# The last feed-forward's gated products by one level of Strassen's scheme, with the weights' block sums kept in DRAM

## The chip, the cores and the metric

One core of a Trainium2 chip. The metric is the device time of one execution in microseconds (us), as the median of several runs. The engines are TensorE (PE; its weight loads are shown apart as PEld), VectorE (DVE), ScalarE (ACT), GpSimd (POOL) and SyncE (SP, which only issues transfers here). They run side by side, each through its own list of instructions in order.

## The reference

Three layers follow each other on 8 x 576 = 4608 tokens of width 512: an attention over 32 memory slots, a feed-forward with 2048 hidden units, and a feed-forward with 768 hidden units, each of them the largest of three products. The last one is what changes:

```python
def _moe_ref(x, w_in, w_out):
    h = x @ w_in
    g = h - np.tanh(h)
    return (g @ w_out).astype(np.float32)

def _moe2_ref(x, w1, w2, w3, w_out):
    h = np.maximum(np.maximum(x @ w1, x @ w2), x @ w3)
    return (h @ w_out).astype(np.float32)
```

`x @ w1`, `x @ w2` and `x @ w3` are the gated products: depth 512, 768 columns each.

## The kernel before

Every 32-bit operand of a large product is split into a high part of type fp32r and the rest, and a product is three matmuls (`mm3`): high x high, high x rest, rest x high. So each factor needs two tiles, made by a copy with a cast and a subtraction.

The tanhshrink feed-forward runs in two passes over the hidden units (`ph` 0 and 1) of 8 blocks `fc` each, over tiles of 288, 320 or 512 tokens; a step is one block of one tile. For a step, `emit_h` makes the hidden values in PSUM (`ps_h`, from `at` and `vw`), `emit_g` takes `h - tanh(h)` on ScalarE and VectorE and splits it (`gh`, the subtraction on GpSimd), and `emit_x` adds its products with `wo` into four PSUM banks (`ps_x`). `emit_h` and `emit_g` run three to four steps ahead. Pass 1 adds the result of pass 0, read from DRAM into `xo`, and writes the sum to DRAM (`xd[1]`). The attention is made in pieces beside pass 0.

Weights come as 64-bit numbers. `conv` turns 512 columns of them into 32 bits: one transfer, one step on ScalarE, five on VectorE, one on GpSimd, and two more where the result is split. Such conversions are background work: `slot()` calls the generators queued in `bg` at a fixed rate per step (`rate[1]`, in quarters per slot, five slots per step). The scheduler behind the program then orders each engine's list by its own estimate of when things are ready. `Paced` ties background instructions of VectorE, ScalarE and TensorE behind the last step's instruction of that engine; GpSimd's and SyncE's are not tied.

The last feed-forward follows pass 1. It walks over nine tiles of 512 tokens. Before it, 9 of the 18 weight blocks (128 of 768 columns of one matrix) are converted during pass 1 and stored in DRAM (`wb_d`); 5 of them are loaded into pool `pre` on GpSimd's queue, the other 4 into pool `wb` as the stage begins. The other 9 and the 6 blocks of the output weights `wz` are converted in the stage itself, during its first tile. `split_x` makes the tile `xh` of split x, in pool `pre` for even tiles and in pool `wb` for odd ones. `emit_max` makes one block of 128 hidden units: for each of the three matrices 12 matmuls of 512 columns into a bank (`ps_w`), then a copy on ScalarE, two maxima on VectorE and the split (`mh`). `emit_out` makes 128 tokens of output: 18 matmuls of 512 columns (`ps_o`) for the tile before, in between the gated products. All 18 + 6 weight blocks stay in SBUF.

Of the kernel before, what the change touches and what calls it, by code (L numbers as in the profile page):

```python
# [7 lines left out]
F32 = mybir.dt.float32  # L8
F32R = mybir.dt.float32r
# [13 lines left out]
def kernel(  # L23
# [76 lines left out]
    cv_p = pool("cv", stack=main)  # L100
# [31 lines left out]
    cv = [cv_p]  # L132
# [228 lines left out]
        yield  # L361


    JP = 3
    wb_d = [dram.tile([P, 3, KD, 2, P], F32, name=f"wb_d{j}") for j in range(JP)]

    def wb_conv(w, j, t=None):
        o = cv_p.tile([P, KD, 2, P], F32R, tag="cs", bufs=1, name="cs") if t is None else t
        src = (moe2_w1, moe2_w2, moe2_w3)[w]
        yield from conv(src[:, j * P:(j + 1) * P].rearrange("(k p) c -> p k c", p=P), o[:, :, 0], o[:, :, 1])  # L370
        if t is None:
            DMA.dma_start(out=wb_d[j][:, w], in_=f(o))
# [35 lines left out]
    fg, bg, ld = Track(), Track(), Track()  # L408
    now, cnt, rate = [0], [0], [10, 8, 4]
# [130 lines left out]
    def chain(*gens):  # L540
        for g in gens:
            yield from g
# [66 lines left out]
    last = ExitStack()  # L609
    pre_p = pool("pre", stack=last, side="right")  # L610
    wb = {(j, w): pre_p.tile([P, KD, 2, P], F32R, name=f"wb{j}{w}") for j, w in ((0, 0), (0, 1), (0, 2), (1, 0), (1, 1))}
    x_t = {}
    xh_p = [pre_p]

    def load_x(i):
        if i < NX:
            x_t[i] = [load_xk(i, kc) for kc in range(2)]

    def load_xk(i, kc):
        xr = pre_p.tile([P, NT], F32, tag="xr", bufs=2, name="xr")  # L620
        DMA.dma_start(out=xr, in_=xd[1][:, kc, i * NT:(i + 1) * NT])
        return xr

    def split_x(i):
        if i < NX:
            xr = x_t[i]
            xh = xh_p[i % 2].tile([P, 2, KD, NT], F32R, tag="xh", bufs=1, name="xh")
            for kc in range(KD):
                S.copy(xh[:, 0, kc], xr[kc])
                V.tensor_sub(xh[:, 1, kc], xr[kc], f(xh[:, 0, kc]))  # L630
                if kc + 2 < KD:
                    xr.append(load_xk(i, kc + 2))
            x_t[i] = xh

    def pre():
        while bg.q:
            bg.step(10 ** 9)
        for j, w in wb:
            G.dma_start(out=wb[j, w], in_=wb_d[j][:, w])
        load_x(0)  # L640
# [9 lines left out]
    wb_p = pool("wb", stack=last2)  # L650
    xh_p.append(wb_p)
    b_p = pool("b", stack=last2)
    cv[0] = b_p
    ps_b = pool("ps_b", PSUM, last2)
    wz = []
    for j in range(1, J):
        for w in range(3):
            if (j, w) not in wb:
                wb[j, w] = wb_p.tile([P, KD, 2, P], F32R, name=f"wb{j}{w}")
                if j < JP:  # L660
                    G.dma_start(out=wb[j, w], in_=wb_d[j][:, w])
                else:
                    bg.add(("wb", j), wb_conv(w, j, wb[j, w]))
    for j in range(J):
        wz.append(wb_p.tile([P, 2, DM], F32R, name=f"wz{j}"))
        bg.add("wz", wz_conv(j, wz[j]))
    m_t = {}
    LR = 6

    def emit_max(i, j):  # L670
        xh = x_t[i]
        pss = []
        bg.need_all(("wb", j))
        for w in range(3):
            for _ in range(LR):
                bg.step(10 ** 9)
            ps = ps_b.tile([P, NT], F32, tag=f"w{w}", bufs=2, name=f"ps_w{w}")
            for kc in range(KD):
                mm3(ps, (wb[j, w][:, kc, 0], wb[j, w][:, kc, 1]), (xh[:, 0, kc], xh[:, 1, kc]), kc == 0, kc == KD - 1)
            pss.append(ps)  # L680
        m = b_p.tile([P, NT], F32, tag="m", bufs=2, name="m")
        S.copy(m, pss[0])
        V.tensor_max(m, pss[1], m)
        V.tensor_max(m, pss[2], m)
        mh = b_p.tile([P, 2, NT], F32R, tag="mh", bufs=12, name="mh")
        S.copy(mh[:, 0], m)
        G.tensor_sub(mh[:, 1], m, f(mh[:, 0]))  # L687
        m_t[i, j] = mh

    def emit_out(i, u):  # L690
        bg.need_all("wz")
        ps = ps_b.tile([P, DM], F32, tag="o", bufs=2, name="ps_o")
        o = slice(u * P, (u + 1) * P)
        for j in range(J):
            mh = m_t[i, j]
            mm3(ps, (mh[:, 0, o], mh[:, 1, o]), (wz[j][:, 0], wz[j][:, 1]), j == 0, j == J - 1)
        ob = b_p.tile([P, DM], F32, tag="ob", bufs=2, name="ob")
        (S.copy if u % 2 else V.tensor_copy)(ob, ps)
        for r in range(0, P, 32):
            b, j = divmod((i * NT + u * P + r) // 32, TJ)  # L700
            dst = out[b * NS:(b + 1) * NS, :].rearrange("(p j) e -> j p e", j=TJ)
            DMA.dma_start(out=dst[j], in_=ob[r:r + 32, :])

    for i in range(NX + 1):
        if i < NX:
            for j in range(J):
                emit_max(i, j)
                if i and j % 3:
                    emit_out(i - 1, j - 1 - j // 3)
                if j == 2:  # L710
                    split_x(i + 1)
                    load_x(i + 2)
        else:
            for u in range(NT // P):
                emit_out(i - 1, u)
    last2.close()
    last.close()

# [29 lines left out]
```

## Time and profile before

| | us |
|---|---|
| median of 3 runs | 1452.91 (1452.79 to 1454.33) |
| profiled execution, span | 1457.4 |
| gated products begin | 843.59 |
| last matmul ends | about 1452.1 |
| PE busy | 1353.8 (93%) |
| DVE, ACT, POOL busy | 629.8, 419.9, 463.2 |

The profiled execution's own time is its span, from its first to its last instruction. Times of single rows are from its start. In rows of instructions a line begins with the start and the duration; matmuls are pipelined, so a row's duration ends with the last matmul's end, and the pace is read from start to start. `L57` is a helper, through which most instructions are recorded: it is the names of the tiles that tell them apart. `PEclk` is the granted clock of TensorE as a share of its full 2.4 GHz.

### The profile page before, as it was taken

The page shows a single profiled execution, that of the slowest core. Times are in us where ns is not written, and L with a number is a line of the kernel's source. Part 1 is how long each engine was busy: PE and PEld are TensorE (multiplying, and loading weights), DVE is VectorE, ACT ScalarE, POOL GpSimd, SP SyncE. Part 2 cuts the span into 40 slices and gives each one's busy share as a digit, 9 for nine tenths or more (in the row PEclk, how much of TensorE's full clock was granted, in tenths as well). Part 3 has the DMA queues.
Part 4 walks back from the last instruction along what each step waited for, and adds up shares of the span by engine and source line. Part 5 has one row for each costly group of instructions (what it writes and reads, how often), then busy time and mean ns, then how long its engine had stood idle before and what let it go on. Part 6 is the DMA issues. An engine that isn't in the chain of part 4 may idle for free.

```text
span 1457.4 us, 21367 instructions
## 1 busy us (share of the span) xinstructions
PE 1353.8 (93%) x8672; PEld 1136.1 (78%) x8672; DVE 629.8 (43%) x1013; ACT 419.9 (29%) x805; POOL 463.2 (32%) x421
## 2 busy tenths in 40 slices
PE   3668798998999899999999999899999999999998
PEld 1457576796887788898989986688888888888886
DVE  4868557676555745533223279621212121121110
ACT  1324234443333343433333233221111111111110
POOL 4446324454323545442323356411111111111110
PEclk9979989998999999999999999999999999999999
DMA  8674746765614536732221253210101011110001
GB/s 217 159 206 136 169 147 185 185 219 144 175 52 170 177 117 215 226 131 98 66 80 61 99 163 101 73 44 15 44 15 51 15 44 30 36 29 15 15 15 44
DMA packets 170130, 152.39 MB, mean 105 GB/s; under 512 B 85040, under 2 KB 144688, under 8 KB 169008
## 3 DMA queue, kind: packets, MB, share of 16 engines
q1 hardware_dynamic: 167968, 145.13, 34.0%
q0 software_dynamic: 2064, 5.90, 1.4%
q8 instruction: 68, 1.11, 0.3%
q14 instruction: 30, 0.25, 0.1%
HBM read 101.97 MB, written 49.02 MB: 104 GB/s over the span
## 4 chain that ended last, share of the span: by engine, by line
PE 77%; DVE 11%; DMA 4%; SPq 2%; issue 2%; ACT 1%; POOL 1%; DVEq 0%; ACTq 0%; POOLq 0%
PE ps_w L57 29%; PE ps_x L57 24%; PE ps_h L57 12%; PE ps_o L57 10%; DVE cva L57 3%; DVE cvb L57 3%; DMA raw<-in_moe_w_in_dram 2%; PE ps_kv L57 2%; SPq L200 1%; DVE s L57 1%; DVE st L57 1%; DMA raw<-in_moe_w_out_dram 1%; DVE vw L57 1%; DVE th L57 1%; DVE qT L57 1%
## 5 line engine op out<-in xcount | busy, mean ns | idle before, releaser
L57 PE MATMUL ps_x<-gh,wo 128*128 128x320 f32 (+2 forms) x2400 | 457.7, 339 | 15.3 <-DVE xo L57 14.0
L57 PE MATMUL ps_w<-xh,wb 128*128 128x512 f32 x1944 | 457.3, 394 | 3.5 <-ACT wb L57 2.7
L57 PEld LDWEIGHTS ps_x<-gh,wo 128*128 128x128 f32 x2400 | 387.0, 194 | 64.2 <-issue 30.0
L57 PEld LDWEIGHTS ps_w<-xh,wb 128*128 128x128 f32 x1944 | 366.0, 189 | 88.5 <-ACT wb L57 3.9
L479 POOL TENSOR_TENSOR gh<-th,gh 128x320 fp32r<-128x320 f32 (+2 forms) x200 | 204.9, 1026 | 322.2 <-ACT gh L57 316.3
L57 PE MATMUL ps_h<-at,vw 128*128 128x256 f32 (+2 forms) x1536 | 259.7, 312 | 34.2 <-DVE th L57 21.7
L57 PEld LDWEIGHTS ps_h<-at,vw 128*128 128x128 f32 x1536 | 232.1, 201 | 63.9 <-DVE th L57 28.4
L57 DVE TENSOR_TENSOR m<-ps_w,m 128x512 f32<-128x512 f32 x108 | 74.4, 690 | 339.6 <-PE ps_w L57 339.6
L687 POOL TENSOR_TENSOR mh<-m,mh 128x512 fp32r<-128x512 f32 x54 | 71.7, 1329 | 443.5 <-ACT mh L57 443.4
L57 DVE TENSOR_TENSOR th<-ps_h,th 128x320 f32<-128x320 f32 (+2 forms) x200 | 107.1, 537 | 230.8 <-ACT th L57 228.8
L57 PE MATMUL ps_o<-wz,mh 128*128 128x512 f32 x648 | 154.4, 391 | 5.3 <-ACT wz L57 5.3
L57 ACT ACTIVATE th<-ps_h 128x320 f32<-128x320 f32 (+2 forms) x200 | 95.1, 478 | 219.4 <-PE ps_h L57 215.0
L57 PEld LDWEIGHTS ps_o<-wz,mh 128*128 128x128 f32 x648 | 121.9, 188 | 32.2 <-ACT wz L57 5.9
L57 ACT CAST gh<-th 128x320 fp32r<-128x320 f32 (+2 forms) x200 | 99.9, 500 | 127.2 <-DVE th L57 109.3
L57 ACT CAST mh<-m 128x512 fp32r<-128x512 f32 x54 | 33.5, 621 | 235.8 <-DVE m L57 235.8
L57 ACT COPY m<-ps_w 128x512 f32<-128x512 f32 x54 | 31.6, 586 | 143.1 <-PE ps_w L57 124.1
L157 POOL TENSOR_TENSOR cva<-cvb,cva 128x512 f32<-128x512 f32 x40 | 52.9, 1324 | 52.3 <-DVE cva L57 51.6
L57 PE MATMUL ps_w<-wi,vT 64*32 64x512 f32 x512 | 46.0, 667 | 11.1 <-DVE s L57 7.7
L57 DVE SCALAR_TENSOR_TENSOR cvb<-raw,cvb 128x512 uint32<-128x512 uint32 x56 | 54.5, 975 | 0.9
L57 DVE TENSOR_TENSOR vw<-ps_w,vw 128x512 fp32r<-128x512 f32 x64 | 41.6, 685 | 28.7 <-ACT vw L57 28.6
L57 ACT ACTIVATE cva<-raw 128x512 f32<-128x512 f32 x56 | 37.5, 671 | 57.4 <-DMA raw<-in_moe_w_in_dram 39.6
L57 DVE SCALAR_TENSOR_TENSOR cva<-raw,cva 128x512 f32<-128x512 uint32 x56 | 45.7, 815 | 1.1
(66 smaller groups left out, 722.1 us busy)
## 6 DMA issues: line engine op xcount, KB each, us to landing
raw<-in_moe_w_out_dram SPq DMA_DIRECT2D x22, 512.0 KB, 3.5
at_d<-at SPq DMA_DIRECT2D x16, 576.0 KB, 4.2
at<-at_d SPq DMA_DIRECT2D x8, 1152.0 KB, 5.1
raw<-in_moe_w_dram SPq DMA_DIRECT2D x18, 512.0 KB, 3.7
xr<-xd SPq DMA_DIRECT2D x36, 256.0 KB, 2.8
out_dram<-ob SPq DMA_DIRECT2D x144, 64.0 KB, 1.7
xd<-xo SPq DMA_DIRECT2D x14, 640.0 KB, 3.7
raw<-in_moe_w_in_dram SPq DMA_DIRECT2D x16, 512.0 KB, 4.7
```

The lines of the kernel that those rows point to most:

```text
L57: i = op(*a, **kw)
L157: G.tensor_add(f(a), f(b), f(a))
L200: q_dma.dma_start(out=t[64 * e + 32 * h:64 * e + 32 * h + 32, r], in_=src[e, h, r])
L479: G.tensor_sub(gh[:, 1], th, f(gh[:, 0]))
L687: G.tensor_sub(mh[:, 1], m, f(mh[:, 0]))
```

## The change

One level of Strassen's scheme (in the form with seven products and shared sums) replaces the gated products. Tokens are taken in 6 groups of 768, in two halves of 384; the depth in two halves of 256; the hidden units in pairs of blocks, `jp`. A unit is one pair and one matrix. Seven products of a 256-deep, 128-wide weight block with a 256-deep, 384-wide token block stand in for eight: 42 matmuls of 384 columns in a unit, 9 units in a group.

- `sw_conv` makes, for each of the 9 units, the seven sums of weight blocks, split, and stores them in DRAM (`sw_d`, 14 KB per partition). That and the 6 blocks of `wz` run as background work in pass 1, at rate 3 instead of 2.
- `first_x` loads the first group's x and makes the seven moving tiles `mv0` to `mv6` with their sums (`xprep`), during the last 16 steps of pass 1. `mv0` to `mv5` lie in pool `pre`, `mv6` in pool `l`. For later groups this is done while the output products of the group before run.
- `load_sw` streams a unit's weights from DRAM into one of four buffers, each group anew; the first three go on GpSimd's queue, the others on SyncE's.
- `unit` runs the seven products on four PSUM banks, three of which take a second product on top, with the shared sums taken out by ScalarE (`p1`, `p5`, `u2`), VectorE and once by GpSimd. Two banks of the eight are kept for the output products.

```diff
-    JP = 3
-    wb_d = [dram.tile([P, 3, KD, 2, P], F32, name=f"wb_d{j}") for j in range(JP)]
...
+    sw_d = [dram.tile([P, 2, 14, P], F32, name=f"sw_d{u}") for u in range(9)]
+    wz_d = [dram.tile([P, 2, DM], F32, name=f"wz_d{j}") for j in range(J)]
+    def sw_conv(jp, w):
+        wsrc = (moe2_w1, moe2_w2, moe2_w3)[w]
+        s = []
+        for h in range(2):
+            t = prep.tile([P, KD, P], F32, tag=f"s{h}", bufs=1, name=f"s{h}")
+            yield from conv(wsrc[:, (2 * jp + h) * P:(2 * jp + h + 1) * P].rearrange("(k p) c -> p k c", p=P), t.rearrange("p k c -> p (k c)"))
+            s.append(t)
+        s0, s1 = s
+        o = prep.tile([P, 2, 14, P], F32R, tag="so", bufs=2, name="so")
+        x = prep.tile([P, 8, P], F32, tag="sx", bufs=1, name="sx")
+        V.tensor_add(x[:, 0:2], s1[:, 0:2], s1[:, 2:4])
+        V.tensor_sub(x[:, 2:4], x[:, 0:2], s0[:, 0:2])
...
+        for lo, n, y in ((0, 4, s0), (4, 2, s1[:, 2:4]), (6, 4, x[:, 0:4]), (10, 4, x[:, 4:8])):
+            S.copy(o[:, 0, lo:lo + n], y)
+            yield
+            G.tensor_sub(o[:, 1, lo:lo + n], y, f(o[:, 0, lo:lo + n]))
+            yield
+        DMA.dma_start(out=sw_d[3 * jp + w], in_=f(o))
...
-    for j in range(JP):
-        for w in range(3):
-            bg.add("wb", wb_conv(w, j), start[1, 0])
+    for u in range(9):
+        bg.add("sw", sw_conv(*divmod(u, 3)), start[1, 0])
+    for j in range(J):
+        bg.add("wz", wz_conv(j), start[1, 0])
...
+    rate[1] = 3
+    NG = 768
...
+    def xprep(x):
+        b11, b12, b21, b22 = x
+        yield from split(B11, b11, V)
+        V.tensor_sub(b11, b12, b11)
+        yield
+        V.tensor_sub(b12, b22, b12)
+        yield
+        yield from split(T3, b12, G)
+        yield from split(T1, b11, V)
+        yield from split(B21, b21, G)
...
-    hooks[start[2, 0] - 14] = [pre]
-    hooks[start[2, 0] - 8] = [lambda: (split_x(0), load_x(1))]
+    hooks[start[2, 0] - 16] = [first_x]
...
+    def load_sw(n, dma=DMA):
+        if n < NU:
+            t = sw_t[n] = get(f"sw{n % 4}")
+            dma.dma_start(out=f(t), in_=sw_d[n % 9])
+    bg.need("x")
+    for n in range(3):
+        load_sw(n, G)
...
+    def unit(n):
...
+        def prod(o, s, x, first, final):
+            for kc in range(2):
+                st = sw[:, :, 2 * s + kc]
+                x0, x1 = mv[x][:, 0, kc], mv[x][:, 1, kc]
+                for k, (lt, rt) in enumerate(((st[:, 0], x0), (st[:, 0], x1), (st[:, 1], x0))):
+                    T.matmul(o, lt, rt, start=first and kc == 0 and k == 0, stop=final and kc == 1 and k == 2, skip_group_check=True)
...
+        prod(A, 0, B11, True, True)
+        S.copy(p1, A)
+        prod(Bk, 5, T3, True, True)
+        prod(Ck, 3, T1, True, True)
+        S.copy(p5, Ck)
+        V.tensor_add(c[:, 3], Bk, p5)
+        prod(Dk, 1, B21, True, True)
+        V.tensor_add(c[:, 0], Dk, p1)
+        prod(A, 4, T2, False, True)
+        S.copy(u2, A)
+        G.tensor_add(c[:, 3], c[:, 3], u2)
+        prod(Ck, 6, B22, False, True)
+        V.tensor_add(c[:, 1], Ck, u2)
+        upd(0)
+        prod(Bk, 2, T4, False, True)
+        load_sw(n + 4)
+        V.tensor_add(c[:, 2], Bk, u2)
+        upd(2)
...
+    for g in range(GR):
+        for n in range(9):
+            unit(9 * g + n)
...
+        outs(g)
```

The order of PE's list in the tanhshrink feed-forward is nearly the same in both programs. On VectorE, early in pass 1 (step 20 of 96), the first tile's x split `xh` stood between the subtractions `th` that feed the next steps:

```order
L57 TENSOR_TENSOR vw<-ps_w,vw 128x512 x2
L57 TENSOR_TENSOR th<-ps_h,th 128x320
L57 TENSOR_TENSOR xh<-xr,xh 128x512 x2
L57 TENSOR_TENSOR vw<-ps_w,vw 128x512 x2
L57 TENSOR_TENSOR th<-ps_h,th 128x320
```

Now the first group's x work stands in the last steps of pass 1, on VectorE:

```order
L57 TENSOR_TENSOR th<-ps_h,th 128x512 x5
L57 TENSOR_TENSOR mv_8456<-xq,mv_8456 128x768
L57 TENSOR_TENSOR xq<-xq 128x768
L57 TENSOR_TENSOR th<-ps_h,th 128x320
L57 TENSOR_TENSOR xq<-xq 128x768
L57 TENSOR_TENSOR th<-ps_h,th 128x320
L57 TENSOR_TENSOR mv_8512<-xq,mv_8512 128x768
```

The x work moved from step 20 to the last 12 steps, and it is again in between the `th` subtractions.

On GpSimd's queue, at the change from pass 1 to the last stage, four loads of `wb` stood behind the last `gh` subtractions:

```order
L479 TENSOR_TENSOR gh<-th,gh 128x320 x8
L661 DMA wb_8432<-wb_d_106 128x1024
L661 DMA wb_8434<-wb_d_107 128x1024
L661 DMA wb_8436<-wb_d_107 128x1024
L661 DMA wb_8438<-wb_d_107 128x1024
```

Now three loads of `sw`, each 3.5 times as large, stand there, and the first unit waits for the first of them:

```order
L498 TENSOR_TENSOR gh<-th,gh 128x320 x2
L644 TENSOR_TENSOR mv_8585<-xq,mv_8585 128x384 x2
L498 TENSOR_TENSOR gh<-th,gh 128x320 x5
L731 DMA sw_8753<-sw_d_105 128x3584
L731 DMA sw_8768<-sw_d_106 128x3584
L731 DMA sw_8769<-sw_d_107 128x3584
```

Before, the weights of the first 5 products were already in SBUF at that point.

On PE, from the last unit of the first group to the first unit of the second (`sw_9092` and `sw_9154` are their weights, `b_` are banks, `mh` and `wz` the output products' factors); before, only `ps_w` and `ps_o` rows of 12 and fewer stood here, all on tiles that had long been made:

```order
L57 MATMUL b_9286<-mv_8558,sw_9092 128x384 x6
L57 MATMUL b_8775<-wz,mh_8755 128x512 x2
L57 MATMUL b_8775<-wz,mh_8756 128x512 x6
L57 MATMUL b_8776<-wz,mh_8755 128x512 x3
L57 MATMUL b_9288<-mv_8585,sw_9092 128x384 x6
L57 MATMUL b_8776<-wz,mh_8755 128x512
L57 MATMUL b_8776<-wz,mh_8756 128x512 x6
L57 MATMUL b_9528<-mv_9389,sw_9154 128x384 x5
L57 MATMUL b_9287<-mv_8754,sw_9092 128x384 x6
L57 MATMUL b_9528<-mv_9389,sw_9154 128x384
L57 MATMUL b_9529<-mv_9394,sw_9154 128x384 x6
```

The next group's tiles (`mv_9389`, `mv_9394`) are used within two output blocks of the last reading of the tiles that they replace.

## Rows read from the trace of the kernel before

**Rows 1.** The page's head: the span, and each engine's busy time.

```profile
span 1457.4 us, 21367 instructions
PE 1353.8 (93%) x8672; PEld 1136.1 (78%) x8672; DVE 629.8 (43%) x1013; ACT 419.9 (29%) x805; POOL 463.2 (32%) x421
```

**Rows 2.** The chain of waits in the last stage: start, duration, engine, tile, count.

```profile
843.59 10.94 PE ps_w L57 x48
...
1005.40 16.81 PE ps_w L57 x72
...
1071.96 16.32 PE ps_w L57 x72
...
1431.68 20.45 PE ps_o L57 x90
```

**Rows 3.** Busy time by stretch: engines with counts, granted clock, DMA share, GB/s.

```profile
843.60:1452.10 608.50, 599.72 (x2592) 487.43 (x2591) 173.13 (x235) 109.57 (x186) 113.00 (x84) 0.99 0.15 43
...
200.00:300.00 100.00, 94.10 (x921) 78.19 (x921) 68.13 (x114) 41.57 (x80) 46.86 (x42) 0.97 0.69 188
600.00:640.00 40.00, 40.00 (x286) 36.97 (x286) 25.46 (x46) 18.61 (x38) 23.67 (x21) 0.99 0.48 163
640.00:680.00 40.00, 40.00 (x255) 34.90 (x254) 11.01 (x19) 13.49 (x27) 11.84 (x12) 1.00 0.33 113
...
842.00:845.00 3.00, 3.00 (x18) 2.74 (x18) 2.48 (x7) 0.00 (x0) 0.00 (x0) 1.00 1.12 415
```

**Rows 4.** PE in order of time, in pass 0 and pass 1.

```profile
409.30 1.93 PE L57 MATMUL ps_x<-gh,wo 128*128 128x320 f32 x12
411.06 1.04 PE L57 MATMUL ps_h<-at,vw 128*128 128x320 f32 x6
...
623.81 1.93 PE L57 MATMUL ps_x<-gh,wo 128*128 128x320 f32 x12
625.58 1.60 PE L57 MATMUL ps_h<-at,vw 128*128 128x256 f32 x12
...
641.83 2.91 PE L57 MATMUL ps_x<-gh,wo 128*128 128x512 f32 x12
644.57 1.60 PE L57 MATMUL ps_h<-at,vw 128*128 128x256 f32 x12
```

**Rows 5.** The page's costliest groups: busy time, mean ns of one, idle before.

```profile
L57 PEld LDWEIGHTS ps_w<-xh,wb 128*128 128x128 f32 x1944 | 366.0, 189 | 88.5 <-ACT wb L57 3.9
...
L57 DVE TENSOR_TENSOR m<-ps_w,m 128x512 f32<-128x512 f32 x108 | 74.4, 690 | 339.6 <-PE ps_w L57 339.6
L687 POOL TENSOR_TENSOR mh<-m,mh 128x512 fp32r<-128x512 f32 x54 | 71.7, 1329 | 443.5 <-ACT mh L57 443.4
...
L57 DVE SCALAR_TENSOR_TENSOR cvb<-raw,cvb 128x512 uint32<-128x512 uint32 x56 | 54.5, 975 | 0.9
...
L57 DVE SCALAR_TENSOR_TENSOR cva<-raw,cva 128x512 f32<-128x512 uint32 x56 | 45.7, 815 | 1.1
```

**Rows 6.** PE and DVE in order of time about 594 us, in pass 1.

```profile
594.22 1.35 DVE L57 TENSOR_TENSOR xh<-xr,xh 128x512 fp32r<-128x512 f32 x2 [6.72 <-ACT xh L57]
...
592.71 1.92 PE L57 MATMUL ps_x<-gh,wo 128*128 128x320 f32 x12
597.22 1.97 PE L57 MATMUL ps_h<-at,vw 128*128 128x320 f32 x6 [2.58 <-DVE th L57]
598.99 3.08 PE L57 MATMUL ps_x<-gh,wo 128*128 128x320 f32 x15
```

**Rows 7.** GpSimd at the end of pass 1, in order of time.

```profile
838.18 0.88 POOL L479 TENSOR_TENSOR gh<-th,gh 128x320 fp32r<-128x320 f32 x1 [1.76 <-ACT gh L57]
839.00 2.16 POOL L661 DMA_DIRECT2D wb<-wb_d  x4
```

**Rows 8.** The page's DMA issues: count, size of each, median us to landing.

```profile
xr<-xd SPq DMA_DIRECT2D x36, 256.0 KB, 2.8
```

**Rows 9.** The page's 40 slices of the span (36.4 us each): GB/s moved.

```profile
GB/s 217 159 206 136 169 147 185 185 219 144 175 52 170 177 117 215 226 131 98 66 80 61 99 163 101 73 44 15 44 15 51 15 44 30 36 29 15 15 15 44
```

More of the change, by code (lines that the diff above doesn't have):

```diff
@@ L608 @@
     wo_s.close()
[L609 to L635, printed above, removed]
+    prep_s, last = ExitStack(), ExitStack()
+    prep = pool("prep", stack=prep_s, side="right")
@@ new lines, with split @@
+    rate[1] = 3
+    NG = 768
+    GR = B * NS // NG
+    NQ = NG // 2
+    B11, T3, T1, B21, T2, B22, T4 = range(7)
+    mv_p, mv = [], {}
+    def split(i, y, eng):
+        t = get("mv6") if i == T4 else mv_p[0].tile([P, 2, 2, NQ], F32R, tag=f"mv{i}", bufs=1, name=f"mv{i}")
+        S.copy(t[:, 0], y)
+        yield
+        if eng is G:
+            for c in range(2):
+                G.tensor_sub(t[:, 1, c], y[:, c], f(t[:, 0, c]))
+                yield
+        else:
+            eng.tensor_sub(t[:, 1], y, f(t[:, 0]))
+            yield
+        mv[i] = t
@@ L636, in pre, with first_x @@
+    def first_x():
         while bg.q:
             bg.step(10 ** 9)
-        for j, w in wb:
-            G.dma_start(out=wb[j, w], in_=wb_d[j][:, w])
-        load_x(0)
-    hooks[start[2, 0] - 14] = [pre]
-    hooks[start[2, 0] - 8] = [lambda: (split_x(0), load_x(1))]
+        prep_s.close()
+        pre_p = pool("pre", stack=last, side="right")
+        mv_p.append(pre_p)
+        x = [(pre_p if t == "xe" else cv_p).tile([P, 1024], F32, tag=t, bufs=n, name="xq")[:, :2 * NQ].rearrange("p (k c) -> p k c", k=2)
+             for t, n in (("raw", 2), ("raw", 2), ("xe", 1), ("cs", 1))]
+        x_load(x, 0)
+        first_x.x = x
+        bg.add("x", xprep(x), start[2, 0] - 12)
@@ L649 @@
     last2 = ExitStack()
[L650 to L653, printed above, removed]
+    l_p = pool("l", stack=last2)
     ps_b = pool("ps_b", PSUM, last2)
[L655 to L663, printed above, removed]
@@ L664 @@
-    for j in range(J):
[L665 to L715, printed above, removed]
+    fresh = {}
+    def lay(tag, shape, dt=F32, p=l_p):
+        fresh[tag] = [shape, dt, p, p.tile(shape, dt, tag=tag, bufs=1, name=tag)]
@@ new lines, in get @@
+    def get(tag):
+        s = fresh[tag]
+        t, s[3] = s[3], None
+        return s[2].tile(s[0], s[1], tag=tag, bufs=1, name=tag) if t is None else t
+    lay("sw0", [P, 2, 14, P], F32R)
+    lay("mv6", [P, 2, 2, NQ], F32R)
+    for i in range(3):
+        lay(f"mh{i}", [P, 2, 2, NG], F32R)
+    for n in ("p1", "p5", "u2"):
+        for i in range(2):
+            lay(f"{n}{i}", [P, NQ])
+    for i in range(2):
+        lay(f"ob{i}", [P, DM])
+    lay("c", [P, 4, NQ])
+    lay("gap", [P, 512])
@@ new lines, in outs, with part, done @@
+    def outs(g):
+        ps = {}
+        def part(u, js):
+            if u not in ps:
+                ps[u] = get(f"b{u % 2}")
+            o = slice(u * P, (u + 1) * P)
+            for j in js:
+                mh = mh_t[j // 2][:, :, j % 2, o]
+                mm3(ps[u], (mh[:, 0], mh[:, 1]), (wz[:, j, 0], wz[:, j, 1]), j == 0, j == J - 1)
+        def done(u):
+            ob = get(f"ob{u % 2}")
+            (S.copy if u % 2 else V.tensor_copy)(ob, ps[u])
+            for r in range(0, P, 32):
+                b, j = divmod((g * NG + u * P + r) // 32, TJ)
+                dst = out[b * NS:(b + 1) * NS, :].rearrange("(p j) e -> j p e", j=TJ)
+                DMA.dma_start(out=dst[j], in_=ob[r:r + 32, :])
+        prep = iter(())
+        if g + 1 < GR:
+            x = [xr[:, k] for k in range(4)]
+            prep = chain(xprep(x), split(T4, x[2], V))
+        for u in range(6):
+            if u == 0:
+                part(0, range(4))
+                part(1, range(4))
+                part(0, range(4, J))
+            elif u == 1:
+                part(1, range(4, J))
+            else:
+                part(u, range(J))
+            done(u)
+            for _ in range(6):
+                next(prep, None)
+        for _ in prep:
+            pass
@@ L716 @@
+    for g in range(GR):
+        for n in range(9):
+            unit(9 * g + n)
+            if n == 0 and g + 1 < GR:
+                xr = get("xr")
+                x_load([xr[:, k] for k in range(4)], g + 1)
+        outs(g)
     last2.close()
```

63 lines of the change are left out of this document (56 added, 7 removed).

## The prediction

> **What bounds the kernel now.** I read the page's head first: TensorE (PE) is busy for 93% of the span [rows 1]. Then the chain of waits, followed backwards from the last instruction. From 843.59 us to the end it is almost only PE in the last feed-forward: pieces of 72 gate products (`ps_w`) and of 18 output products (`ps_o`), each starting where the one before ends, up to 1452.13 [rows 2]. That is 608.5 us for 1944 + 648 = 2592 matmuls of 512 columns; the busy times of that stretch put PE at 599.7 of 608.5 and no other engine above 173 [rows 3]. At the fast pace (16.32/72 = 226.7 ns [rows 2]) 2592 would take 587.6, so 21 us are lost: some 15 before 940 us, where the weights are still being converted, the rest in the slower pieces (16.81/72 = 233.5 ns). So in this stage time is bought by taking columns away from PE, and by moving the conversions out.
>
> **What a matmul costs by its columns.** The changed products have 384 columns, which no row shows. The rows on both sides of it: 12 matmuls of 320 columns take 625.58 - 623.81 = 1.77 us, 12 of 512 take 644.57 - 641.83 = 2.74 [rows 4]; per matmul 147 and 228 ns, in the last stage 226.7 at best. One column is 1/2.4 ns at the full clock, which these stretches were granted (0.99 to 1.00 [rows 3]); what remains is 13.8 and 13.4 ns. So 384 columns cost 160 + 13.3 = **173.3 ns**, if nothing else sets the pace.
>
> **The change part by part.**
> *Gate products.* Per 768 tokens before: 324 matmuls of 512 columns. After: 9 units (3 pairs of column blocks, 3 matrices) of 7 products, 2 halves of depth, 3 matmuls each: 378 of 384 columns. For 6 groups: 2268 x 0.1733 = **393.1 us**. Upper bound: the 233.5 ns pace. By the code, the slow pieces are those whose weights and moving tiles lie in different pools: the x tiles change pool from one token tile to the next, and so does the pace [rows 2]. After the change six of seven products pair weights in pool `l` with moving tiles in pool `pre`. That would add up to 6.8 ns to 6/7 x 2268 = 1944 matmuls, 13 us. The other way speaks a 320-column row of the first pass over the hidden units: there the weights lay in pool `wo`, on the other side from `gh`, and 12 took 411.06 - 409.30 = 1.76, no slower than the row at 623.81 [rows 4]. 384 is nearer to 320 than to 512, so I take 0.
> *Output products.* 648 of 512 columns as before, at 20.45/90 [rows 2]: **147.2 us**. Sum on PE 540.3.
> *Evictions.* A unit lasts 42 x 0.1733 = 7.3 us. VectorE (DVE) gives it four 384-column sums out of PSUM and two 768-column maxima. A 512-column one takes 0.69 [rows 5]; at most 4 x 0.69 + 2 x 1.04 = 4.8 us. GpSimd (POOL) has one add of 384, at most 1.33 [rows 5]. ScalarE has three copies. All hidden under the 7.3. The products of a unit are ordered so that a bank is written again two or more products (2 us) after it is read. Cost 0; if that cover failed, it would be paid 54 times (a rival below).
> *Between groups.* Seven moving tiles exist once, so each is overwritten while unit 8 still runs; the scheduler puts output products and the next group's first unit in between, as the last of the orders shown with the change has it. From the last read of the T3 tile to its next use PE has about 10 us of work; the refill is a copy on ScalarE, two POOL subtractions (2 x at most 1.33 [rows 5]) behind two others: about 7 us. I put 0.5 us on each of 6 boundaries, **3 us**; bounds 0 and 12.
> *Start of the stage.* Before, the first weights are there at 843.59. Now the first sw tile (128 x 14336 B = 1.835 MB) is loaded on POOL's queue behind the last `gh` subtraction, which ends at 839.06; the four `wb` loads of before stand in the same place, at 839.00 [rows 7], and move at 415 GB/s while they run [rows 3]. A load of 256 KB lands after 2.8 us [rows 8], of which 0.6 is that rate; with the other 2.2, 839.0 + 2.2 + 1.835/0.415 = 845.6; PE waits **2 us**. After a wait of that kind PE ran at half clock: from 597.22 six 320-column matmuls took 1.77 us instead of 0.88, and the next 15 took 3.08 in their row where 15 x 0.147 + 0.16 = 2.4 would be usual [rows 6], 1.6 lost; I add **1.9**. Weights of the next units, `wz` and the next x arrive at 415 GB/s just ahead of their use (14.5 MB by about 876; unit 4 starts at 875). Cost 3.9; bounds 2 and 8.
> *The stage before it.* Its PE order stays as it was. Removed: the wait at 594. DVE stood 6.72 us before the first x split (`xh`), which the scheduler had put early, ahead of a tanhshrink subtraction; PE, done at 592.71 + 12 x 0.147 = 594.47, stood 2.7 us and then lost the 1.6 [rows 6]: **-4.3**. Added: 24 weight conversions instead of 9, and the sums for them. Five DVE steps each, the two dearest 0.98 and 0.82 [rows 5], so at most 4.2 x 24 = 102 us of DVE in some 265 us, 38%, beside the 11.0 of 40 that the stage needs without them [rows 3]: about two thirds busy. From 600 to 640 DVE was as busy (25.5 of 40) and PE lost nothing [rows 3]. But DVE's order also has the new x splits, which wait for a load that waits for the last `wz_d` store; that can repeat the 594 case once. I take **+3**; bounds 0 and 16 (a rival).
>
> **The sum.** Last stage 540.3 + 3 + 3.9 = 547.2 against 608.5: -61.3. Stage before: -1.3. Together -62.6. The profiled execution's span is 1457.4, the median of the runs 1452.91, 4.5 less, and I keep that distance. Span after 1394.8, predicted median **1390.3 us**.
>
> **The rivals.**
> (a) *Pools far apart slow the 384-column products as they slow the 512-column ones* [rows 2]. For it: the address pattern fits every piece of the last stage. Against it: the 320-column row [rows 4]. +13 us: 1403.
> (b) *Conversions crowd the stage before.* From 200 to 300 us DVE is busy 68 of 100 and PE 94 [rows 3]; 6% of 265 us is 16 instead of the 3 I took, +13: 1403. Against it: 600 to 640 us.
> (c) *The weight load sets the pace*: every matmul loads its own 128 x 128 weights, 189 ns each [rows 5]. At 189 per matmul the products take 428.7, +36: 1426. Against it: 320-column matmuls run at 147 with loads of the same size [rows 4]. The Trainium skill, page "TensorE: Matmul & The Clock Gate", section "Back-to-back issue gap", goes further and gives a stream of load and matmul pairs about 81 ns at 128 columns and 131 at 512; by an estimate between them (114 ns at 384) the count would matter more than the columns, the gate products would go from 255 to 259 us and the change would buy nothing on PE. This case's rows disagree: 227 ns at 512 and 147 at 320.
> (d) *Hand-overs.* If each of 54 units waited 1 us for a bank: +54, 1444. Against it: the cover above.
> (e) *The weight stream cannot keep up, and the kernel gets slower.* Each group now moves 9 x 1.835 MB of weights, 1.57 of x and 1.57 of output: 19.7 MB in 90.6 us, 217 GB/s over the whole stage. Only two of the page's 40 slices reach more, 219 and 226, and the first 17 average 170 [rows 9]. At 170 a group takes 115.6 us and the stage 150 us more: 1541. It turns slower than before below 195 GB/s (6 x 101 us). Against it: those slices are full of small packets; 4 KB rows ran at 415 [rows 3] and the sw rows are 14 KB.
>
> **How the numbers follow.** Forecast 0.54; (a) 0.20; (b) 0.13; (c) 0.04; (d) 0.04; (e) 0.05. Low end: no added cost in the stage before (-3), none between groups (-3), a start of 2 (-1.9): 1382. High end: (a) and (b) together: 1416, which leaves out (c), (d) and (e), 0.13. The range is 1382 to 1416. Two in a thousand is about what a measurement here can tell from no change; below that I put 0.01, slower 0.04 (most of (e)), faster 0.95.
>
> **What the profile after would show.** Matmuls with 384 columns starting 173 ns apart (180 in (a), 189 in (c)); the last stage about 548 us long at a granted clock near 1.0; a wait of PE of about 2 us on the first `sw` load and half clock right after; no DVE wait for `xr` in the stage before; DVE near two thirds in that stage with PE still at 99%; the DMA row near 217 GB/s in the last 15 slices and sw landing within some 7 us; in (e) PE would wait for `sw` in every unit, in (d) for DVE or ScalarE. The prediction is wrong if PE waits inside units, or if the stage before it grows by more than 10 us.

## The result, and the profile after

The changed kernel takes **1403.82 us** (median of 4 runs, 1402.22 to 1404.89); the kernel before, on the same chip, 1453.62 (4 runs, 1452.79 to 1455.13). The ratio is 0.9657, 95% interval 0.9639 to 0.9675: 3.4% faster. The forecast was 1390.3, the range 1382 to 1416. So the time lies in the range, 13.5 us above the forecast, at the place where rivals (a) and (b) stood (1403).

| | before | after |
|---|---|---|
| median | 1453.62 | 1403.82 |
| profiled execution: span | 1457.4 | 1402.7 |
| last product of pass 1 ends | 843.59 | 835.28 |
| last matmul ends | 1452.12 | 1397.85 |
| last stage, from the one to the other | 608.5 | 562.6 |

The page of the changed kernel: its head, and five of its costliest groups (busy time, mean ns of one, idle time before them and what ended most of it).

```profile
span 1402.7 us, 22759 instructions
PE 1302.9 (93%) x8996; PEld 1166.1 (83%) x8996; DVE 818.0 (58%) x1259; ACT 478.2 (34%) x937; POOL 586.1 (42%) x505
...
L57 PE MATMUL b<-mv,sw 128*128 128x384 f32 x2268 | 410.2, 340 | 5.3 <-DMA sw<-sw_d 5.3
L57 PEld LDWEIGHTS b<-mv,sw 128*128 128x128 f32 x2268 | 403.4, 189 | 9.5 <-DMA sw<-sw_d 3.9
...
L57 PE MATMUL b<-wz,mh 128*128 128x512 f32 x648 | 157.7, 393 | 3.0 <-POOL mh L796 2.3
...
L796 POOL TENSOR_TENSOR mh<-m,mh 128x768 fp32r<-128x768 f32 (+1 forms) x36 | 67.5, 1896 | 50.3 <-ACT mh L57 50.3
```

Against [rows 1] PE is busy 51 us less, with 324 matmuls more, since 1944 of 512 columns became 2268 of 384. DVE has 188 us more. PE waited for two things in the new stage: 5.3 us for weights, and 3.0 ahead of output products, of which 2.3 were for `mh`.

Now the places. First the two stages, then two stretches at the start of the last one (busy time and count of PE, PEld, DVE, ACT, POOL, then granted clock, DMA share, GB/s).

```profile
516.19:835.12 318.93, 317.72 (x2128) 286.80 (x2126) 209.17 (x331) 146.01 (x290) 192.91 (x171) 1.00 0.52 184
835.12:1397.90 562.78, 554.43 (x2918) 523.25 (x2916) 275.64 (x368) 143.37 (x268) 169.92 (x120) 0.99 0.59 212
...
836.00:838.00 2.00, 0.00 (x0) 0.00 (x0) 0.99 (x2) 0.00 (x0) 0.00 (x0) 0.88 1.02 430
838.93:841.50 2.57, 2.57 (x8) 2.57 (x9) 0.00 (x0) 0.25 (x1) 0.00 (x0) 0.50 0.99 420
```

Pass 1 carries 24 conversions and their sums with DVE 66% busy (209.17 of 318.93), and PE still at 99.6%: rival (b) did not happen. The stream moves 212 GB/s over the stage, as in the estimate of (e) (217), and PE is at 98.5%. Right after its first wait PE has the lower of its two clocks (0.50, 1.2 GHz): 8 matmuls in 2.57 us, some 320 ns each.

The start of the last stage in the chain of waits of the changed kernel (start, duration, what):

```profile
830.31 0.82 POOL gh L498
831.14 7.75 DMA sw<-sw_d
...
838.93 19.13 PE b L57 x94
858.06 12.57 DMA sw<-sw_d
...
870.76 32.34 PE b L57 x180
```

SyncE's queue there (start, duration, transfers):

```profile
836.76 0.61 SPq L731 DMA_DIRECT2D sw<-sw_d  x1
837.42 7.88 SPq L741 DMA_DIRECT2D wz<-wz_d  x6
849.88 7.20 SPq L670 DMA_DIRECT2D xr<-xd  x4
858.06 18.44 SPq L731 DMA_DIRECT2D sw<-sw_d  x4
```

And PE in order of time; what stands in brackets is the wait ahead of the row:

```profile
838.93 30.22 PE L57 MATMUL b<-mv,sw 128*128 128x384 f32 x156 [3.64 <-DMA sw<-sw_d]
870.76 2.36 PE L57 MATMUL b<-mv,sw 128*128 128x384 f32 x12 [1.62 <-DMA sw<-sw_d]
...
888.10 21.35 PE L57 MATMUL b<-mv,sw 128*128 128x384 f32 x120
909.29 2.68 PE L57 MATMUL b<-wz,mh 128*128 128x512 f32 x11
...
922.66 0.73 PE L57 MATMUL b<-wz,mh 128*128 128x512 f32 x2 [0.40 <-POOL mh L796]
```

The first weights are asked for when `gh` is done (831.14) and land 7.75 us later. The fifth unit's are asked for at 858.06, behind the six `wz` and the four x transfers on the same queue, and take 12.57: a second wait. And the pace: 120 products in 909.29 - 888.10 = 21.19 us, **176.6 ns** each, not 173.3.

Taken apart by the distances between starts of PE's matmuls (a distance more than 30 ns over the pace is counted as a stall), the 562.6 us of the last stage are:

| term | forecast | measured | difference |
|---|---|---|---|
| 2268 gate products | 173.3 ns: 393.1 | 176.4 ns: 400.1 | +7.0 |
| 648 output products | 227.2 ns: 147.2 | 228.5 ns: 148.1 | +0.9 |
| start: wait and low clock | 2 + 1.9 | 3.6 + 2.6 | +2.3 |
| fifth unit's weights | 0 | 1.9 | +1.9 |
| six hand-overs between groups and the end | 3 | 1.1 + 4 x 0.9 + 1.5 = 6.2 | +3.2 |
| sum | 547.2 | 562.5 | +15.3 |

### The profile page after: what moved, and what is told of

Read it like the earlier page. It is cut to its first block, busy times and chain, and to the rows that moved or that the text cites. A ratio compares the mean times of both kernels' runs of the same rounds, so it can differ in the third digit from the quotient of the medians.

```text
span 1402.7 us, 22759 instructions
## 1 busy us (share of the span) xinstructions
PE 1302.9 (93%) x8996; PEld 1166.1 (83%) x8996; DVE 818.0 (58%) x1259; ACT 478.2 (34%) x937; POOL 586.1 (42%) x505
## 4 chain that ended last, share of the span: by engine, by line
PE 72%; DVE 12%; DMA 7%; POOL 4%; ACT 2%; issue 2%; SPq 1%; DVEq 0%; ACTq 0%; POOLq 0%
PE b L57 32%; PE ps_x L57 22%; PE ps_h L57 12%; DMA sw<-sw_d 3%; DVE cva L57 2%; PE ps_w L57 2%; POOL mv L644 2%; DMA raw<-in_moe_w_in_dram 2%; PE ps_kv L57 2%; DVE cvb L57 2%; DVE s L57 1%; DVE st L57 1%; DMA xo<-xd 1%; DVE th L57 1%; POOL mh L796 1%
## 5 line engine op out<-in xcount | busy, mean ns | idle before, releaser
L57 PE MATMUL b<-mv,sw 128*128 128x384 f32 x2268 | 410.2, 340 | 5.3 <-DMA sw<-sw_d 5.3
L57 PEld LDWEIGHTS b<-mv,sw 128*128 128x128 f32 x2268 | 403.4, 189 | 9.5 <-DMA sw<-sw_d 3.9
L57 PE MATMUL b<-wz,mh 128*128 128x512 f32 x648 | 157.7, 393 | 3.0 <-POOL mh L796 2.3
L781 POOL TENSOR_TENSOR c<-c,u 128x384 f32<-128x384 f32 x36 | 40.0, 1112 | 277.1 <-ACT u L57 277.1
L57 PEld LDWEIGHTS b<-wz,mh 128*128 128x128 f32 x648 | 120.3, 188 | 29.7 <-POOL mh L796 4.3
L57 ACT COPY p<-b 128x384 f32<-128x384 f32 x108 | 51.7, 478 | 164.8 <-PE b L57 159.3
L57 DVE TENSOR_TENSOR c<-b,u 128x384 f32<-128x384 f32 x72 | 39.8, 553 | 86.2 <-PE b L57 86.2
L796 POOL TENSOR_TENSOR mh<-m,mh 128x768 fp32r<-128x768 f32 (+1 forms) x36 | 67.5, 1896 | 50.3 <-ACT mh L57 50.3
L57 DVE TENSOR_TENSOR m<-c,m 128x768 f32<-128x768 f32 x72 | 73.8, 1024 | 4.1
L644 POOL TENSOR_TENSOR mv<-xr,mv 128x384 fp32r<-128x384 f32 x30 | 45.0, 1526 | 28.8 <-ACT mv L57 28.8
```

The source lines that it names most:

```text
L57: i = op(*a, **kw)
L644: G.tensor_sub(t[:, 1, c], y[:, c], f(t[:, 0, c]))
L781: G.tensor_add(c[:, 3], c[:, 3], u2)
L796: e.tensor_sub(mh[:, 1, h, o], y, f(mh[:, 0, h, o]))
```

## The experiments

What was open after this: why the pace is 176.4 and not 173.3, whether the stream of weights has a part in it, what the start and the hand-overs are worth, and how much of the gain is the seven products' own. All kernels ran beside the kernel before, whose median was between 1452 and 1454 us each time. Where one run is given, the last stage in its trace says more than its total: the four totals of the changed kernel alone lie 2.7 us apart.

### The pace: where the moving tiles begin

Theory A is the prediction's rival (a) in a sharper form. In a partition of SBUF the weight buffers and `mv6` begin at a multiple of 64 bytes, `mv0` to `mv5` 32 bytes off one. (Before, pool `pre` and pool `wb` stand to each other in the same way.) By A that offset slows the products. Theory P takes rival (a) at its word: the two pools lie far apart. Theory S: the stream of weights into SBUF slows the reading of the operands. An unused strip as the last tile of pool `pre` moves the six tiles by 32 bytes and changes no instruction's place:

```diff
+        if i == B22 and len(mv_p) == 1:
+            mv_p.append(mv_p[0].tile([P, 8], F32, name="shim"))
```

> The changed kernel, with an unused strip of 32 bytes behind the tiles of pool `pre`, so that the moving tiles mv0 to mv5 start on a multiple of 64 bytes as the weights do (before, 32 bytes off); nothing else moves. In the changed kernel the 384-column products start 176.6 ns apart with mv0 to mv5 and 175.2 with mv6, which lies in the weights' pool; forecast was 173.3. Theory A (the offset of 32 bytes between moving tile and weights slows the pair): all products at 173.3, the last stage 562.7 - 7 = 556 us, median 1404 - 7 = 1397. Theory P (the two pools lie far apart in SBUF): no change, 176.6 and 1404. Theory S (the weight stream from DRAM disturbs PE's reads): no change here either.

Measured: 1399.54 us (4 runs, 1398.15 to 1402.64), ratio 0.9631 (0.9609 to 0.9654). The page's group of gate products:

```profile
L57 PE MATMUL b<-mv,sw 128*128 128x384 f32 x2268 | 404.9, 338 | 5.5 <-DMA sw<-sw_d 5.5
```

PE in order of time:

```profile
870.12 3.16 PE L57 MATMUL b<-mv,sw 128*128 128x384 f32 x12 [1.82 <-DMA sw<-sw_d]
...
888.77 21.00 PE L57 MATMUL b<-mv,sw 128*128 128x384 f32 x120
909.61 2.67 PE L57 MATMUL b<-wz,mh 128*128 128x512 f32 x11
```

The same 120 products take 20.84 us, 173.7 ns each. By tile: `mv0` to `mv5` 173.3 ns (176.6 in the changed kernel), `mv6`, which did not move, 176.0 (175.2). With `mv0` to `mv5` that is the forecast's pace to a tenth, and the address alone gave it: P and S, by which nothing would change here, fall as the cause of the 3.3 ns. The stage shortened by only 3.4 us, though the pace gave 6.2: PE reached the fifth unit earlier than its weights and stood there for 3.6 us in all instead of 1.9, with the lower clock behind it (12 products in 3.16 us), and the hand-overs grew from 0.9 to 1.15 each.

The same strip with 88 elements in place of 8 puts all seven tiles and the weights at the same place within 512 bytes:

> As the run with 32 bytes, but 352 bytes, which puts mv0 to mv5 at the same place in a block of 512 bytes as the weights. Theory A on a grid of 64 bytes: 173.3 ns as with 32 bytes. If only a coarser grid counts (128 to 512 bytes): 173.3 here and 176.6 with 32 bytes. Theories P and S: 176.6 in both.

Measured: 1402.67 us in one run. The pace is 173.7 with every tile, `mv6` too; 4.7 us instead of 1.9 are lost around the fifth unit. Counted within 512 bytes, the weights and `mv6` begin at 128 in all three kernels, `mv0` to `mv5` at 480, 448 and 128. So the place counts, but not by the residue of 64 alone: `mv6` stood at the same address in all three and took 175.2, 176.0 and 173.7. Which rule of addresses it is stays open.

The kernel before with the same strip in its pool `pre`:

> The kernel before, with the same strip of 32 bytes behind pool `pre`: the even x tiles and five weight blocks then start on a multiple of 64 bytes like the rest. Theory A: the slow pieces vanish, all 512-column products of the steady part at 226.6 ns instead of 226.6 and 233 in turn; about half of 2592 matmuls by 6 ns, 7 us less: 1446. Theory P: pieces stay at 226.6 and 233 in turn, 1453. Theory S says nothing here, as there is no stream in that stage.

Measured: 1448.46 us in one run, last stage 605.7 instead of 608.5. Its chain of waits:

```profile
835.64 10.93 PE ps_w L57 x48
...
997.24 16.50 PE ps_w L57 x72
...
1030.25 16.75 PE ps_w L57 x72
...
1063.32 16.32 PE ps_w L57 x72
```

The piece that answers to the slow one of [rows 2] (16.81) takes 16.50, 229 ns a matmul instead of 233.5; the other kind of slow piece, with the pools the other way round, stays at 16.75; the fast one is 16.32 as before. So the slow pieces of the kernel before answer to the same 32 bytes, which remove a part; theory A's forecast for this kernel, 226.6 everywhere, did not come out. This run also dates the profiled execution of before: the same instructions reach the gated products at 835.64, not at 843.59 [rows 2].

### The weight stream

S alone: only the first four units' weights are loaded and used over and over, so that 50 of the 54 loads are left out.

```diff
-    NU = 9 * GR
+    NU = 4
...
-        sw = sw_t.pop(n)
+        sw = sw_t[n % 4]
```

> The changed kernel, but only the first four units' weights are loaded, and every unit uses one of these four buffers again: 50 of 54 loads of 1.8 MB are left out, so the gated products are not those of the reference. Theory S (the stream disturbs PE's reads): the products go from 176.6 to 173.3 ns. Theories A and P: still 176.6. All: PE's wait of 1.9 us for the fifth load goes, and nothing else if the stream is hidden: last stage 562.7 - 2 = 561, total about 1402. If the stream cost more than that one wait, the stage is shorter by the difference.

Measured: 1403.37 us in one run, last stage 560.7. The page's group of gate products:

```profile
L57 PE MATMUL b<-mv,sw 128*128 128x384 f32 x2268 | 409.9, 340 | 3.7 <-DMA sw<-sw_d 3.7
```

The stretch from 840 to 1396 us (columns as above, the last is GB/s):

```profile
840.00:1396.00 556.00, 552.94 (x2914) 522.66 (x2914) 273.72 (x364) 143.58 (x268) 170.04 (x120) 1.00 0.15 47
```

With 47 GB/s in place of 212 the pace is the same, 176.4 ns. Only the wait for the fifth unit is gone, 1.9 us. S falls here too, and with it what was left of rival (e): leaving out some 92 MB of transfers saved 1.9 us, all at the start.

### The start

The first unit's weights as seven loads of 256 KB, in the order of its products, so that the first product need not wait for the whole 1.8 MB:

```diff
+            if n == 0:
+                for s in (0, 5, 3, 1, 4, 6, 2):
+                    dma.dma_start(out=f(t)[:, :, 2 * s:2 * s + 2], in_=sw_d[0][:, :, 2 * s:2 * s + 2])
```

> The changed kernel, but the first unit's weights are loaded in seven pieces of 256 KB in the order of the seven products, on the same queue and at the same place. In the changed kernel PE waited 3.6 us for the whole 1.8 MB and then ran its first 17 products at half clock, 2.6 us more. If the wait is for the size of that load: the first piece lands by about 834, PE goes on at 835.1 with a wait under 0.5 us and at full clock, the last stage is 6 us shorter (557). If the wait is for the queue (the issue or the first data come late): the wait stays near 3.6 us. A later unit may then wait some 1 to 2 us for its own load, since PE gets there sooner.

Measured: 1406.72 us in one run, last stage 565.7, **3.2 us longer**. PE in order of time:

```profile
834.76 7.04 PE L57 MATMUL b<-mv,sw 128*128 128x384 f32 x39
845.18 22.91 PE L57 MATMUL b<-mv,sw 128*128 128x384 f32 x114 [3.37 <-DMA sw<-sw_d]
871.79 13.38 PE L57 MATMUL b<-mv,sw 128*128 128x384 f32 x67 [3.71 <-DMA sw<-sw_d]
```

The first wait is gone, and it came back as 6.2 us at the second unit (3.37 of standing, the rest the lower clock) and 5.3 at the fifth instead of 1.9. From 835 to 875 the queues moved 403 GB/s here and 413 from 834 to 875 in the changed kernel, DMA share 1.01 and 1.02: until some 875 us the queues are full in both kernels.

But the pieces have a price of their own. GpSimd's queue, first in the changed kernel, then here:

```profile
831.14 1.69 POOL L731 DMA_DIRECT2D sw<-sw_d  x3
...
830.25 5.08 POOL L733 DMA_DIRECT2D sw<-sw_d  x7
835.34 1.13 POOL L735 DMA_DIRECT2D sw<-sw_d  x2
```

The stretch from 834 to 838 us, in the same order (columns as above):

```profile
834.00:838.00 4.00, 1.28 (x9) 1.02 (x7) 2.55 (x5) 0.00 (x0) 0.00 (x0) 0.94 0.98 416
...
834.00:838.00 4.00, 4.00 (x25) 4.00 (x24) 2.11 (x5) 0.87 (x2) 2.46 (x4) 1.00 0.91 273
```

The second unit's weights were asked for 5.1 us after the first piece, where it had been 0.6 us, and while the pieces ran, with rows of 1 KB in place of 14 KB, the queues moved 273 GB/s instead of 416. So the run shows that this way of starting earlier moves the wait and makes it longer. How much of it the full queues would have cost without the pieces' slower transfer, no run separates.

What can be changed besides is the order of the bytes. The second group's x behind the weights of units 5 to 8:

```diff
-            DMA.dma_start(out=y, in_=xd[1][:, kc:kc + 2, g * NG + h * NQ:g * NG + (h + 1) * NQ])
+            i = DMA.dma_start(out=y, in_=xd[1][:, kc:kc + 2, g * NG + h * NQ:g * NG + (h + 1) * NQ])
+            if g:
+                tc.add_manual_dep(i.ins, sw_i[0].name, mybir.DependencyInfo(mybir.DependencyClass.NoSync, mybir.DependencyReason.DATA), reason="x later")
...
-            if n == 0 and g + 1 < GR:
+            if n == 3 and g + 1 < GR:
```

> The changed kernel, with the next group's x (1.6 MB) loaded behind the weights of the fifth to eighth unit instead of ahead of the fifth. In the changed kernel PE waited 1.9 us at 869 us for the fifth unit's weights, whose load was issued behind x. If the queue's order makes that wait: it goes, the last stage is 1.9 us shorter (561). If it is the total of what has to be moved by then: the wait stays at 1 us or more.

Measured: 1400.61 us in one run, last stage 560.3. SyncE's queue in this kernel:

```profile
848.51 23.72 SPq L733 DMA_DIRECT2D sw<-sw_d  x4
872.28 2.37 SPq L670 DMA_DIRECT2D xr<-xd  x4
```

PE in order of time:

```profile
837.41 31.44 PE L57 MATMUL b<-mv,sw 128*128 128x384 f32 x168 [3.65 <-DMA sw<-sw_d]
868.69 1.09 PE L57 MATMUL b<-wz,mh 128*128 128x512 f32 x4
```

All of the first four units run through (168 products in one row), and the wait for the fifth is gone. In this run the lower clock after the first wait cost 1.6 us, in others up to 2.7; that spread is not explained.

### The hand-overs

At each of them PE waited for GpSimd's `mh`, whose widest subtraction (768 columns) takes 1.9 us. That one subtraction on DVE:

```diff
-            for q, nq, e in ((0, 2, G), (3, 1, G), (2, 1, V)):
+            for q, nq, e in ((0, 2, V), (3, 1, G), (2, 1, V)):
```

> The changed kernel, with the 768-column subtraction of each hidden block's split on VectorE (about 1.0 us) instead of GpSimd (1.9 us). In the changed kernel PE waits 0.9 to 1.1 us at each of the five changes of group and 1.5 us at the last output products, and the releaser named there is that subtraction. If it makes the wait: about 1 us each is gone, the last stage 5 to 6 us shorter (557). If the chain behind it on VectorE (the maxima and the last 384-column part of the split) ends as late: the wait stays or grows, 562 or more.

Measured: 1400.32 us in one run, last stage 558.7. All that PE itself waited for in the stage (in total, times, longest):

```profile
PE b L57 <- DMA sw<-sw_d: 5.1, 2, 3.7
PE b L57 <- DVE ob L57: 0.5, 1, 0.5
PE b L57 <- ACT mh L57: 0.4, 1, 0.4
PE b L57 <- DVE mh L57: 0.3, 1, 0.3
```

The five waits at the changes of group are gone, 4.7 us; the end, whose last outputs have nothing behind them, takes 2.1 instead of 1.5. Net 3.9.

### The conversions alone

The kernel before with all its weight conversions in pass 1 at rate 3, stored and loaded, and no Strassen:

```diff
-    JP = 3
+    JP = J
...
+    for j in range(J):
+        bg.add("wz", wz_conv(j), start[1, 0])
...
+    rate[1] = 3
...
-                if j < JP:
-                    G.dma_start(out=wb[j, w], in_=wb_d[j][:, w])
-                else:
-                    bg.add(("wb", j), wb_conv(w, j, wb[j, w]))
+                (DMA if j > 2 else G).dma_start(out=f(wb[j, w]), in_=wb_d[j][:, w])
```

> The kernel before with one part of the change alone: all 18 gate weight blocks and the 6 blocks of wz are converted during pass 1 (rate 3) and loaded from DRAM when the last stage begins; the products stay 512 columns wide and eight to a block (no Strassen). If the gain splits as the two traces say: pass 1 gives nothing or up to 3 us back, the last stage loses its 12 us or so of waits before 940 us and keeps 2592 matmuls at about 229 ns, 594 + 2 us against 608.5; total 1454 - 12 to 15 = 1439 to 1442, and the step from there to 1404 is the seven products' own. Rival: the conversions were hidden well enough, and 1450 or more comes out, so that all of the gain is the products'.

Measured: 1448.86 us (10 runs, 1445.56 to 1451.86), ratio 0.9974 (0.9960 to 0.9987). What PE waited for from 506 us to the end of pass 1 (in total, times, longest):

```profile
PE ps_h L57 <- DVE th L57: 5.3, 3, 3.7
PE ps_x L57 <- DVE xo L57: 3.6, 5, 1.5
```

DVE's early x split in this kernel:

```profile
593.43 1.36 DVE L57 TENSOR_TENSOR xh<-xr,xh 128x512 fp32r<-128x512 f32 x2 [3.68 <-ACT xh L57]
```

The last stage loses 12.9 us (595.6), but pass 1 grows by 8.5: PE's waits for DVE went from 3.3 to 8.9 us in this stretch, and the early x split of [rows 6] is still there, now in a denser DVE. The waits make 5.6 of the 8.5 us; the rest was not taken apart. So neither forecast came out whole: the last stage is as the first had it, and pass 1 takes most of it back. In the changed kernel, without that split, pass 1 carries the same conversions and is 2.7 us shorter than before. That it is the split which makes this difference is likely but not shown, since no run has the early conversions and a late split with the old products. Of the 46.0 us by which the last stage shrank, 12.9 come with the moved conversions and, by subtraction, 33 with the seven products.

### Together

The strip, the later x, `wz` moved behind the weights of the sixth unit and the subtraction on DVE, in one kernel; once also with the first load in pieces. What is new in them is the place of `wz`:

```diff
-    for j in range(J):
-        DMA.dma_start(out=f(wz[:, j]), in_=wz_d[j])
...
+            if g == 0 and n == 1:
+                for j in range(J):
+                    i = DMA.dma_start(out=f(wz[:, j]), in_=wz_d[j])
+                    tc.add_manual_dep(i.ins, sw_i[0].name, mybir.DependencyInfo(mybir.DependencyClass.NoSync, mybir.DependencyReason.DATA), reason="wz later")
```

> Five edits on the changed kernel at once: the 32-byte strip (pace 173.7 instead of 176.4 ns), the first unit's weights in seven 256-KB pieces, the second x load and the wz loads queued behind the weights of units 5 to 8, and the 768-column mh subtraction on DVE. If each saving stands: last stage 562.7 - 6.2 (pace) - 6.2 (idle and half clock at the start) - 1.9 (fifth unit) - 4.3 (boundaries) = 544, span 1384, median about 1386. Rival: the start is bound by bytes, so that what the first pieces save is paid as a wait for the second unit's weights (6.25 us with pieces alone): then the stage is about 550 and the median about 1392; and it is worse than the same kernel with the first load whole.

> As the run with five edits, but the first unit's weights in one load again. Start as in the changed kernel (idle about 3.7, half clock about 2.6): last stage 562.7 - 6.2 - 1.9 - 4.3 = 550, span 1390, median about 1392. Rival: as with the strip alone, half of the pace is given back to waits at the start (the faster products reach the third to fifth unit before their weights): stage 553 to 554, median about 1396.

Measured: with the first load whole **1391.74 us** (4 runs, 1391.11 to 1394.78), ratio 0.9574 (0.9560 to 0.9589); in pieces 1393.11 (5 runs, 1388.5 to 1396.79), ratio 0.9578 (0.9556 to 0.9599). Between the two no difference can be told. The first is 12 us below the changed kernel. PE in order of time, with the load in pieces:

```profile
836.57 7.70 PE L57 MATMUL b<-mv,sw 128*128 128x384 f32 x42
847.58 25.71 PE L57 MATMUL b<-mv,sw 128*128 128x384 f32 x132 [3.31 <-DMA sw<-sw_d]
```

And with the load whole:

```profile
842.51 32.04 PE L57 MATMUL b<-mv,sw 128*128 128x384 f32 x174 [3.70 <-DMA sw<-sw_d]
874.39 1.08 PE L57 MATMUL b<-wz,mh 128*128 128x512 f32 x4
```

In pieces, the rival named in its expectation took place, though no kernel is clearly the worse: 6.4 us at the second unit, last stage 550.1. Whole, it went as its first forecast said: the last stage is 549.3 us, of which 393.9 are gate products at 173.7 ns, 147.8 output products, 3.7 and 1.7 at the start, 2.1 at the end. That is the forecast's 547.2 with its terms nearly in place. In the traces the last stage is 3.4 us shorter with the strip alone, 2.3 with the later x and 3.9 with the subtraction, 9.6 in sum, and 13.3 with all of them. Most of the 3.7 us more is what the strip alone gave back, 1.8 at the fifth unit and 1.3 at the hand-overs, where nothing takes it back any more. (By the totals it is 11.0 against 12.1 us, but two of the three single edits were run once.)

## Why the prediction was right, and where it was off

**The trade of columns against counts: right.** The forecast of -61.3 us for the last stage became -46.0, with the mechanism as told: 2268 matmuls of 384 columns in place of 1944 of 512, evictions hidden, no unit waiting for a bank (rival (d) is dead: all of PE's stalls fall on the start, the fifth unit, the hand-overs and the end). Rival (c) is dead too: the weight loads are still 189 ns each on the page, and the products start 176 apart, 173 with the strip. The pace rule of the Trainium skill (page "TensorE: Matmul & The Clock Gate", section "Back-to-back issue gap") put beside it in the prediction does not hold here either: it took some 173 ns at best with 384 columns, where an estimate between its two figures gives 114.

**The pace of the gate products: mis-sized, +7.0.** "384 is nearer to 320 than to 512, so I take 0" is the step that failed: the surcharge is 3.3 ns at 384 columns with `mv0` to `mv5`. The 320-column row of the first pass was read rightly, and it is no row of other addresses: `gh` begins there at a multiple of 64 bytes and `wo` 32 bytes off one, the same offset. What differs is the width. With the same tiles 512 columns are slow in the first pass, and this stood in the trace of before:

```profile
465.29 2.96 PE L57 MATMUL ps_x<-gh,wo 128*128 128x512 f32 x12
468.09 1.59 PE L57 MATMUL ps_h<-at,vw 128*128 128x256 f32 x12
```

12 of them take 468.09 - 465.29 = 2.80 us, 233.3 ns each, against 228.3 in the second pass [rows 4], where `gh` and `wo` both begin at a multiple of 64. With 320 columns the two passes give 146.9 and 146.7 ns. (Between the passes `wo` also changes its pool; that it is the 32 bytes is shown for the last stage alone.) So an offset that cost nothing at 320 columns cost 3.3 ns at 384 and some 5 to 7 at 512. Rival (a) had the right pairs of tiles, took the 6.8 ns of 512 columns whole, and so priced them at +13, about double; its cause, the distance of the pools, does not explain the 3.3 ns, since the strip left the pools where they are.

**The start: mis-sized, +2.3, and the fifth unit, +1.9.** The rate was right (413 to 430 GB/s), the instant was not: the load was priced as landing 6.6 us after its issue (2.2 + 1.835/0.415) and took 7.75, with two more loads on the same queue and a third on SyncE's beside it, and pass 1 ended sooner after the last `gh`. "Just ahead of use" was the step for the later units; it was written without the order on SyncE's queue, where ten transfers stood ahead of the fifth unit's weights. Its own two numbers, 14.5 MB by 876 us and a use at 875, already put those bytes behind their use, and the wait was taken as 0.

**The hand-overs: +3.2.** 0.5 each was put on the refill of the moving tiles; what PE waited for was the other tile there, `mh` on GpSimd, 0.9 to 1.5 each. The cost is within its bounds (0 to 12), the cause is not the one named.

**Pass 1: right within 1.4.** Forecast -1.3; from 521.82 (before) and 516.19 (after), the same product in both, to its end it took 2.7 us less. The wait at 594 is gone (-4.3) and DVE is two thirds busy, so some 1.6 of the +3 for the conversions was needed: PE's waits for DVE there sum to 2.0 us, 1.2 of them new.

**The distance from span to median: wrong, and hidden by luck.** The profiled execution of before was a late one: it reached pass 1 5.6 us after the changed kernel, in a part where the two programs are alike, and the kernel before with the strip shows it again (835.64 against 843.59). A run's time is its span plus 1.7 us (1404.43 for the span of 1402.7), so that execution took some 1459, not 1452.91. The forecast subtracted 4.5 for this and counted no gain ahead of pass 1; the trace shows 5.6 gained there and nothing to subtract. The two errors cancel by chance: of the miss of 13.5, the last stage is +15.3, pass 1 -1.4, and some -0.5 lies behind the last matmul.

**The chances.** That the time came out at 1403 is not rival (a) alone, nor (b): about half of the last stage's miss is the pace, the other half three small waits. The hand-overs stayed within their bounds; the start with the fifth unit, 8.1 us, came out just over its bounds of 2 to 8. The upper end of the range was made by (a) and (b) together. (b) did not take place, and without its 13 us the range would have ended at 1403, just below the measured time: that the time lies inside is in part luck.

## What to carry to other kernels

When fewer columns are bought with more data from DRAM, the steady rate is soon checked, and here the cost was at the start: draw up the bytes queue by queue until the stream is ahead, and put what is used last behind what is used first. Where the queues are full, a first load in smaller pieces can move the wait to the next unit, and the pieces may themselves be slower (273 against 416 GB/s here). When matmuls of the same shape run at two paces, compare where in SBUF their two operands begin. And a surcharge that is absent at one width need not be absent at the next: look for the same tiles at every width that the trace has.

## What the runs showed of the hardware

- The pace of these fp32r matmuls depends on where in a partition the moving tile and the weights begin. With the tiles of one pool 32 bytes lower and no instruction changed, 384 columns went from 176.6 to 173.3 ns and 512 columns from 233.5 to 229; with both operands in one pool 512 columns took 226.7. At 320 columns tiles with the same offset showed nothing of it (146.9 against 146.7). The rule behind it was not found; all operands at the same place within 512 bytes gave 173.7 with every tile.
- After PE had stood for 3.3 to 3.7 us, its granted clock was the lower one (0.50 of 2.4 GHz in its row): the next matmuls of 384 columns started some 320 ns apart, and 12 to 20 of them cost 1.6 to 3 us over their usual pace. After 1.6 us of standing it was not lower in the changed kernel (12 products in 2.36 us), and after 1.8 in the strip's run it was (3.16).
- One core's queues moved 413 to 430 GB/s at the start of the last stage, where most bytes came in rows of 14 KB, and 273 while seven loads of 256 KB with rows of 1 KB ran. A load of 1.8 MB on SyncE's queue landed in 7.3 us in the median.
